# Three buffers for sums, x and v, three pairs of gates, and products five chunks behind: a long convolution beside a gated feed-forward layer

## The chip, the core and the metric

The kernel runs on one core of a Trainium2 chip. The metric is device time in microseconds (us). Three runs of the kernel before the change took 3942.79, 3947.40 and 3949.95 us; the median is 3947.4 us.

## The reference

Two blocks follow each other. B is 4, S is 12480, D is 128, the hidden width DFF is 2048; everything is float32.

```python
# block 1: a long convolution with a gate
h_filt = (np.maximum(pos_emb @ w1, 0.0) @ w2) * np.exp(-0.01 * pos)[:, None]
u = x * v
y = irfft(rfft(u, n=2*S) * rfft(h_filt, n=2*S))[:S]      # along the sequence, per column
z = x * y
# block 2: on the 49920 rows of z
h = z @ w_in                 # 128 -> 2048
out = (h * np.cos(h)) @ w_out   # 2048 -> 128
```

## The kernel before

**The convolution** is a Fourier transform written as matrix products in stages. For each of the four batches there are a first stage (f1, `f1_units`, 64 units), a second with the product by the filter's transform (f2, `f2_units`, 48 units), a third (i1, `i1_units`, 64 units) and a last (i2, `i2_units`, 30 units). Each i2 unit reads one tile `tm` of 312 KB from DRAM, multiplies the result by x (`i2_out`, L518, on VectorE) and stores it in `zd`. While i2 of batch b runs, `u_units` makes u = x*v of batch b+1: per unit it loads `xt` and `vt` (L385), multiplies in two halves (L404) and writes sums and differences into `slots` (L410). All of that arithmetic is GpSimd's (POOL). All DMAs are issued by SyncE (SP), in order, so an issue that waits holds up every later one.

**The feed-forward layer** (`moe_*`) runs beside the convolution from 343 us on. Rows come in 97 tiles of 128 x 4, and each tile has 16 chunks of 128 hidden columns; 1552 chunks in all. Chunk i is: the product with w_in (`moe_up`, L132, into a PSUM bank `ph`), a rounding on ScalarE (ACT, L753), a subtraction on VectorE (DVE, L754), a sine on ACT (L759) and a product on DVE (L760) that gives the gate `gt`. The product with w_out is a Strassen-like scheme on pairs of chunks: `moe_sums` makes four sums `ts` of a pair on POOL (L768, L771, L772), and `moe_down` multiplies gates and sums by seven combinations of weights (L785): the first half of a pair into `acca` (three products, the last of them from the sum made by L771), the second into `accb` (four products). After a tile's last pair `moe_evict` combines the accumulators into `ot`; `moe_back` transposes them into `ob`, `moe_store` writes them out. `moe_load` reads a tile of z into `zb`, `moe_turn` transposes it into `at`.

**The order** is written out by hand (`manual_schedule`, L985 to L1017). Step i issues `moe_up` of chunk i, then `moe_down` of chunk i - LAG (LAG is 6), then the sine and product of chunk i-1, then, where chunk i-1 closes a pair, its sums; then transposes if they are due (in at chunk 3, out at chunk 8). After that it issues pieces of convolution as long as these are owed:

```python
            owed += 1.0
            while owed > 0.0:
                owed -= next(conv, owed)
```

An f2 unit counts for 2.9 steps, an i2 unit for 3.5 steps in batch 0, for 3.0 in batches 1 and 2 and for 1.5 in batch 3. When the convolution has run out (at about 3160 us), the rest of the chunks runs alone; I call this the tail. There every second `ph` comes from the convolution's PSUM banks (`late`).

**Buffers.** `gt` has four pairs, `ts` two, `zb`, `ot` and `ob` one each. PSUM: `acca` and `accb` take a bank each, `ph` three; the convolution has two banks in batch 0 and three afterwards. In f2 the scratch `t` has one buffer. In `u_units`, a `bufs` of 2 gives two `xt` and one `vt`; the loads of a unit are issued `bufs - 2` units ahead.

Of the kernel before, what the change touches and what calls it, by code (L numbers as in the profile page):

```python
# [9 lines left out]
F32 = mybir.dt.float32  # L10
# [7 lines left out]
P = 128  # L18
# [15 lines left out]
def kernel(  # L34
# [71 lines left out]
    NROWS = B * NG * R  # L106
    NALL = 1 + math.ceil((NROWS - R) / P)
    assert G == 2 * UA and H % UA == 0 and N2 % G == 0
    LAG = 6
    WCOL = 256  # L110

    dram = ctx.enter_context(tc.tile_pool(name="dram", bufs=1, space=DRAM))
# [351 lines left out]
    def f2_product(pool, ps, h, k1, whole):  # L464


        y = parts[0:N2, :, k1:k1 + 2, :, :].rearrange("p r k b i -> p r b (k i)")
        t = pool.tile([N2, 2, CB, 4], F32, name="t", bufs=1 + whole)
        uu = ps[0:N2, :].rearrange("p (r b j) -> p r b j", r=2, j=4)
        if whole:  # L470
            for r, (dst, hh) in enumerate(((y, h[:, :, :, :]), (t[:, :, :, :], h[:, ::-1, :, :]))):
                u = uu[:, r]
                twice = bass.AP(tensor=u.tensor, offset=u.offset,
                                ap=[u.ap[0], [0, 2], *u.ap[1:]])
                nc.vector.tensor_tensor(dst, twice, hh, op=ALU.mult)  # L475
                yield
        for r, op in ((0, ALU.subtract), (1, ALU.add)):
            if not whole:
                nc.vector.tensor_tensor(y[:, r], uu[:, 0], h[:, r], op=ALU.mult)
                yield  # L480
                nc.vector.tensor_tensor(t[:, r], uu[:, 1], h[:, 1 - r], op=ALU.mult)
            nc.gpsimd.tensor_tensor(y[:, r], y[:, r], t[:, r], op=op)  # L482
            yield
# [83 lines left out]
    def u_units(b, bufs, u, engine, side="left"):  # L567

        with tc.tile_pool(name="xv", bufs=bufs, side=side) as pool:
            tiles = {}  # L570

            def before(j):
                tiles[j] = u_load(pool, bufs, b, j * UA)

            def after(j, _):
                for half in range(2):
                    u_multiply(tiles[j], half, engine(j, half))
                    yield
                if j == H // UA - 2:
                    clear_gap(u)  # L580
                u_sums(u, tiles.pop(j), j * UA, (nc.gpsimd, nc.gpsimd if b else nc.vector))
                yield

            yield from units(H // UA, U_STEPS, before, lambda j, ps, i: None, after, 3,
                             ahead=bufs - 2)
# [107 lines left out]
    def inverse_units(bank, b):  # L693

        if b + 1 == B:
            yield from i2_units(bank, b, 3)
            return
        new = u_units(b + 1, 2, slots[0:R, :, :, :],  # L700
                      lambda j, half: nc.gpsimd,
                      side="right" if b else "left")
        parts = 4 if b == 0 else 2
        for i, steps in enumerate(i2_units(bank, b, 2)):
            if i > 2 * parts:
                for _ in range(i % parts > 0 if b == 0 else 1 + i % 2):
                    next(new, None)
            yield steps * (FIRST_STEPS if b == 0 else I2U_STEPS) / I2_STEPS
        yield from new
# [18 lines left out]

    def moe_load(pool, n):
        m, row = rows_of(n), first_row(n)  # L730
        zb = pool.tile([P, G, D], F32, name="zb", bufs=1)
        nc.sync.dma_start(zb[0:m, :, :], zd[row:row + m, :, :])
        zbs[n] = zb

    def moe_turn(pool, n):
        m = rows_of(n)
        zb = zbs.pop(n)
        pt = ps_h.tile([P, BANK], F32, name="ph")
        for i in range(G):
            transpose(pt[:, i * m:(i + 1) * m], zb[0:m, i, :], ident)  # L740
        at = pool.tile([D, BANK], F32, name="at")
        nc.scalar.copy(out=at[:, 0:G * m], in_=pt[:, 0:G * m])
        ats[n] = at
# [18 lines left out]
    def moe_sums(pool, n, gt):  # L762

        half = G // 2 * rows_of(n)
        ts = pool.tile([P, 4, BANK // 2], F32, name="ts")
        t = [ts[:, i, 0:half] for i in range(4)]
        b11, b21 = gt[:, 0, 0:half], gt[:, 1, 0:half]
        nc.gpsimd.tensor_tensor(  # L768
            ts[:, 0:2, 0:half], gt[:, :, half:2 * half],
            gt[:, 0, 0:2 * half].rearrange("p (h n) -> p h n", h=2), op=ALU.subtract)  # L770
        nc.gpsimd.tensor_tensor(t[2], t[1], b11, op=ALU.add)  # L771
        nc.gpsimd.tensor_tensor(t[3], b21, t[2], op=ALU.subtract)  # L772
        return b11, b21, gt[:, 1, half:2 * half], t
# [16 lines left out]
    def moe_evict(pool, n, second, ot=None):  # L790
        r = rows_of(n)
        acc = sums.pop((n, second))

        def twice(a):
            return bass.AP(tensor=a.tensor, offset=a.offset, ap=[a.ap[0], [0, 2], a.ap[1]])

        if not second:
            ot = pool.tile([P, 6, P], F32, name="ot", bufs=1)
            nc.scalar.copy(out=ot[:, 2, 0:r], in_=acc[:, 0, 0:r])
            nc.vector.tensor_tensor(ot[:, 0:2, 0:r], acc[:, 1:3, 0:r], twice(ot[:, 2, 0:r]),  # L800
                                    op=ALU.add)
            return ot
        nc.vector.tensor_tensor(ot[:, 2:4, 0:r], acc[:, 0:2, 0:r], twice(ot[:, 0, 0:r]),
                                op=ALU.add)
        nc.vector.tensor_tensor(ot[:, 4:6, 0:r], acc[:, 2:4, 0:r], ot[:, 2:4, 0:r], op=ALU.add)
        nc.vector.tensor_tensor(ot[:, 0, 0:r], acc[:, 1, 0:r], ot[:, 2, 0:r], op=ALU.add)
        return ot

    def moe_back(pool, n, ot):
        m = rows_of(n)  # L810
        pt = ps_h.tile([P, BANK], F32, name="ph")
        places = pt[:, :].rearrange("p (h i e d) -> p h e i d", h=2, e=2, d=CB)
        for i, block in enumerate((1, 4, 5, 0)):
            transpose(places[0:m, i // 2, i % 2], ot[:, block, 0:m], ident)
        ob = pool.tile([P, 2, UA * D], F32, name="ob", bufs=1)
        nc.scalar.copy(out=ob[0:m, :, :].rearrange("p h n -> p (h n)"), in_=pt[0:m, :])
        return ob

    def moe_store(n, ob):
        row = first_row(n)  # L820
        while row < first_row(n + 1):
            b, g, n1 = row // R // NG, row // R % NG, row % R
            count = min(R - n1, first_row(n + 1) - row)
            first, _, second, _ = n2s(g)
            start = out[b * S + n1 * N2 + first, :]
            at = row - first_row(n)
            nc.sync.dma_start(
                bass.AP(tensor=start.tensor, offset=start.offset,
                        ap=[[N2 * D, count], [(second - first) * D, 2], [1, UA * D]]),
                ob[at:at + count, :, :])  # L830
            row += count

    with tc.manual_schedule():
# [143 lines left out]
        def load(n):  # L977
            while made[0] * R < first_row(n + 1):
                next(conv)
            moe_load(mpool, n)  # L980
# [4 lines left out]
        steps = [(n, c) for n in range(NALL) for c in range(NFC)]  # L985
        hidden, pairs, gates, ots, obs = {}, {}, {}, {}, {}
        for i in range(len(steps) + LAG):
            if i < len(steps):
                n, c = steps[i]
                if n == 0 and c == NFC // 2:  # L990
                    load(1)
                if c == NFC - 4 and n + 2 < NALL:
                    load(n + 2)
                if c % 2 == 0:
                    pairs[i] = mpool.tile([P, 2, BANK], F32, name="gt", bufs=4)
                hidden[i] = moe_up(mpool, n, c, pairs[i - c % 2])
            if i >= LAG:
                pn, pc = steps[i - LAG]
                moe_down(pn, pc // 2, pc % 2, *gates[i - LAG - pc % 2])
                if pc >= NFC - 2:  # L1000
                    ots[pn] = moe_evict(mpool, pn, pc % 2, ots.get(pn))
            if 0 <= i - 1 < len(steps):
                moe_act(*hidden.pop(i - 1))
                pn, pc = steps[i - 1]
                if pc % 2:
                    gates[i - 2] = moe_sums(mpool, pn, pairs.pop(i - 2))
            if i < len(steps):

                if c == (3 if n else NFC - 2) and n + 1 < NALL:
                    moe_turn(mpool, n + 1)  # L1010
                if c == NFC // 2 and n - 1 in ots:
                    obs[n - 1] = moe_back(mpool, n - 1, ots.pop(n - 1))
                if c == NFC // 2 + 2 and n - 1 in obs:
                    moe_store(n - 1, obs.pop(n - 1))
# [3 lines that stand above are left out]
# [30 lines left out]
```

## Time and profile before

| quantity | value |
|---|---|
| median of three runs | 3947.4 us |
| the profiled execution, its own time | 3949.47 us |
| its span (first to last instruction) | 3947.6 us |
| TensorE (PE) busy | 3703.9 us (94%) |
| DVE busy | 2903.3 us (74%) |
| POOL busy | 2838.1 us (72%) |
| ACT busy | 2281.0 us (58%) |
| mean granted clock of PE | 0.983 |

Busy time is an average over stages that are limited by different things, so it has to be read by stage: 350 to 610 us is i2 of batch 0, 620 to 1205 us is f1, f2 and i1 of the next batch, 1215 to 1505 us its i2, and so on; 3020 to 3160 us is the last i2 and from there on the tail. The profile names a wait by the instruction that waits and the one that released it. The end of a matmul is modelled, so durations of PE are better read from start to start.

### The profile page before, as it was taken

Reading aid. Unit: us, or ns where it says so; the run is one execution under the profiler, and the core shown is the slowest. Engines: PE = TensorE matmul, PEld = TensorE weight load, DVE = VectorE, ACT = ScalarE, POOL = GpSimd, SP = SyncE. Lnnn points to the kernel's source line nnn. Section 1 sums busy time; section 2 is a strip of 40 time slices with the busy share of each in tenths; the row PEclk is TensorE's granted clock in tenths of the full one; section 3 lists DMA queues with packets and bytes.
Section 4 is the critical chain, followed back from the end, with each engine's and each line's share of the span. In section 5 each row is a group of like instructions: output and inputs, shape, how many; then the busy total and the mean of one; then the engine's idle time right before and its main releaser. Section 6 shows DMA issues by size and latency. Waiting matters only on the chain.

```text
span 3947.6 us, 101170 instructions
## 1 busy us (share of the span) xinstructions
PE 3703.9 (94%) x40298; PEld 2595.6 (66%) x40298; DVE 2903.3 (74%) x5722; ACT 2281.0 (58%) x4660; POOL 2838.1 (72%) x3361
## 2 busy tenths in 40 slices
PE   7898999999999889999999889999999999999999
PEld 6776766655576656655577566655577766666666
DVE  8887777777776557787776456777777577777777
ACT  5756666655554446655555345655555367776776
POOL 7667996688746776688846776588854477878777
PEclk9999999999999999999999999999999999999999
DMA  5253541122203541122202551022202500000000
GB/s 159 78 165 114 158 142 29 36 69 73 62 13 106 141 130 36 29 71 70 66 19 79 142 145 39 24 70 73 68 23 73 163 27 18 23 20 21 23 18 19
DMA packets 209709, 279.59 MB, mean 71 GB/s; under 512 B 17111, under 2 KB 146535, under 8 KB 209111
## 3 DMA queue, kind: packets, MB, share of 16 engines
q1 hardware_dynamic: 209239, 273.12, 24.1%
q8 instruction: 320, 5.24, 0.6%
q14 instruction: 150, 1.23, 0.1%
HBM read 193.64 MB, written 79.42 MB: 69 GB/s over the span
## 4 chain that ended last, share of the span: by engine, by line
PE 67%; POOL 11%; DMA 5%; DVE 5%; issue 2%; ACT 1%; SPq 1%; POOLq 0%; ACTq 0%; DVEq 0%
PE ph L132 23%; PE cv L132 18%; PE accb L785 14%; PE acca L785 10%; DMA tm<-td 4%; POOL ts L768 4%; PE ph L136 2%; POOL ts L771 2%; POOL ts L772 2%; DVE gt L760 2%; DVE gt L754 1%; POOL xt L404 1%; POOL slots L482 1%; POOL slots L410 1%; ACT gt L753 1%
## 5 line engine op out<-in xcount | busy, mean ns | idle before, releaser
L753 ACT ACTIVATE gt<-ph 128x512 int32<-128x512 f32 (+1 forms) x1339 | 797.7, 596 | 1347.3 <-PE ph L132 1231.3
L768 POOL TENSOR_TENSOR ts<-gt 128x512 f32<-128x512 f32 (+2 forms) x784 | 998.4, 1273 | 791.4 <-PE accb L785 737.1
L754 DVE SCALAR_TENSOR_TENSOR gt<-ph,gt 128x512 f32<-128x512 f32 (+1 forms) x1339 | 918.9, 686 | 791.1 <-ACT gt L753 779.3
L132 PE MATMUL ph<-at,w_in_sb 128*64 128x512 f32 (+1 forms) x5356 | 1414.0, 601 | 78.6 <-DVE gt L760 56.8
L759 ACT ACTIVATE gt<-gt 128x512 f32<-128x512 f32 (+1 forms) x1568 | 973.8, 621 | 32.1 <-DVE gt L754 32.1
L760 DVE TENSOR_TENSOR gt<-ph,gt 128x512 f32<-128x512 f32 (+1 forms) x1339 | 907.4, 678 | 0.3
L785 PEld LDWEIGHTS acca<-gt,w_out_sb 128*64 128x64 f32 x6272 | 410.0, 137 | 435.7 <-issue 425.3
L785 PE MATMUL accb<-ts,w_out_sb 128*64 128x128 f32 (+2 forms) x9408 | 655.1, 273 | 0.0
L772 POOL TENSOR_TENSOR ts<-gt,ts 128x256 f32<-128x256 f32 (+2 forms) x784 | 571.1, 728 | 61.5
L771 POOL TENSOR_TENSOR ts<-ts,gt 128x256 f32<-128x256 f32 (+2 forms) x784 | 570.6, 728 | 61.5
L785 PEld LDWEIGHTS accb<-ts,w_out_sb 128*64 128x64 f32 x9408 | 549.3, 138 | 0.0
L785 PEld LDWEIGHTS accb<-gt,w_out_sb 128*64 128x64 f32 x3136 | 236.7, 137 | 439.3 <-issue 437.3
L132 PEld LDWEIGHTS ph<-at,w_in_sb 128*64 128x64 f32 x5356 | 362.8, 138 | 186.1 <-issue 50.9
L785 PE MATMUL acca<-gt,w_out_sb 128*64 128x128 f32 (+2 forms) x6272 | 483.3, 273 | 0.0
L132 PE MATMUL cv<-slots,tm 96*40 96x128 f32 (+1 forms) x3840 | 286.6, 293 | 88.4 <-DMA tm<-td 81.8
L482 POOL TENSOR_TENSOR slots<-slots,t 120x256 f32<-120x256 f32 x384 | 278.9, 737 | 57.9 <-DVE t L475 35.9
L785 PE MATMUL acca<-ts,w_out_sb 128*64 128x128 f32 (+1 forms) x3136 | 311.7, 273 | 2.3 <-POOL ts L771 2.1
L785 PE MATMUL accb<-gt,w_out_sb 128*64 128x128 f32 (+1 forms) x3136 | 312.4, 273 | 0.0
L132 PEld LDWEIGHTS cv<-slots,tm 96*40 96x40 f32 (+1 forms) x3840 | 240.0, 130 | 106.8 <-DMA tm<-td 92.7
L132 PE MATMUL cv<-at,w_in_sb 128*64 128x512 f32 (+1 forms) x916 | 234.7, 591 | 0.0
L404 POOL TENSOR_TENSOR xt<-xt,vt 104x256 f32<-104x256 f32 x228 | 169.4, 750 | 68.4 <-DMA vt<-in_v_dram 65.0
L785 PEld LDWEIGHTS acca<-ts,w_out_sb 128*64 128x64 f32 x3136 | 205.2, 138 | 3.1 <-POOL ts L771 3.1
(145 smaller groups left out, 4109.6 us busy)
## 6 DMA issues: line engine op xcount, KB each, us to landing
h<-hd SPq DMA_DIRECT2D x144, 240.0 KB
tm<-td SPq DMA_DIRECT2D x96, 312.0 KB
xt<-in_x_dram SPq DMA_DIRECT2D x120, 208.0 KB
vt<-in_v_dram SPq DMA_DIRECT2D x120, 208.0 KB
xs<-in_x_dram SPq DMA_DIRECT2D x120, 208.0 KB
zd<-xs SPq DMA_DIRECT2D x119, 208.0 KB
zb<-zd SPq DMA_DIRECT2D x96, 256.0 KB
w<-wd SPq DMA_DIRECT2D x144, 116.2 KB
```

The costliest lines, as they stand in the source:

```text
L132: nc.tensor.matmul(dst[lo:hi], left[:, lo:hi], right, start=start, stop=stop)
L136: nc.tensor.transpose(dst, src, ident[0:n, 0:n])
L404: engine.tensor_tensor(xt[:, half, :], xt[:, half, :], vt[:, half, :], op=ALU.mult)
L482: nc.gpsimd.tensor_tensor(y[:, r], y[:, r], t[:, r], op=op)
L753: nc.scalar.activation(turns, ph[:, 0:m], AF.Identity, bias=phase)
L754: nc.vector.scalar_tensor_tensor(out=part, in0=ph[:, 0:m], scalar=phase, in1=turns, op0=ALU.add, op1=ALU.subtract)
L759: nc.scalar.activation(part, part, AF.Sin, scale=scale)
L760: nc.vector.tensor_tensor(part, ph, part, op=ALU.mult)
L768: nc.gpsimd.tensor_tensor(ts[:, 0:2, 0:half], gt[:, :, half:2 * half], gt[:, 0, 0:2 * half].rearrange("p (h n) -> p h n", h=2), op=ALU.sub ...
L771: nc.gpsimd.tensor_tensor(t[2], t[1], b11, op=ALU.add)
L772: nc.gpsimd.tensor_tensor(t[3], b21, t[2], op=ALU.subtract)
L785: nc.tensor.matmul(acc[h * CB:(h + 1) * CB, place, 0:r], w_out_sb[:, pair, weight, :], right[:, h * r:(h + 1) * r], start=(pair == 0 and i ...
```

## The change

It does the following:

- `LAG` is 5, and within a step `moe_down` (with `moe_evict`) is issued ahead of `moe_up`; `gt` has three pairs, `ts` three buffers.
- `t` in f2 has two buffers.
- `u_units` of the later batches gets `bufs=3`: three `xt`, two `vt`, and loads one unit ahead.
- The transposes in are issued at chunk 8, directly ahead of the transposes out, and take a PSUM bank of the convolution.
- `zb` and `ob` share one buffer (`tile`); `ot` has four blocks in place of six, and the evictions of `accb` are reordered so that the last adds in place.

```diff
-    LAG = 6
+    LAG = 5
...
-        t = pool.tile([N2, 2, CB, 4], F32, name="t", bufs=1 + whole)
+        t = pool.tile([N2, 2, CB, 4], F32, name="t", bufs=2)
...
-        new = u_units(b + 1, 2, slots[0:R, :, :, :],
+        new = u_units(b + 1, 3, slots[0:R, :, :, :],
...
-        zb = pool.tile([P, G, D], F32, name="zb", bufs=1)
+        zb = pool.tile([P, G, D], F32, name="tile", bufs=1)
...
-        pt = ps_h.tile([P, BANK], F32, name="ph")
+        pt = bank()
...
-        ts = pool.tile([P, 4, BANK // 2], F32, name="ts")
+        ts = pool.tile([P, 4, BANK // 2], F32, name="ts", bufs=3)
...
-            ot = pool.tile([P, 6, P], F32, name="ot", bufs=1)
+            ot = pool.tile([P, 4, P], F32, name="ot", bufs=1)
...
-        nc.vector.tensor_tensor(ot[:, 4:6, 0:r], acc[:, 2:4, 0:r], ot[:, 2:4, 0:r], op=ALU.add)
         nc.vector.tensor_tensor(ot[:, 0, 0:r], acc[:, 1, 0:r], ot[:, 2, 0:r], op=ALU.add)
+        nc.vector.tensor_tensor(ot[:, 2:4, 0:r], acc[:, 2:4, 0:r], ot[:, 2:4, 0:r], op=ALU.add)
...
-        for i, block in enumerate((1, 4, 5, 0)):
+        for i, block in enumerate((1, 2, 3, 0)):
...
-        ob = pool.tile([P, 2, UA * D], F32, name="ob", bufs=1)
+        ob = pool.tile([P, G, D], F32, name="tile", bufs=1)
...
         for i in range(len(steps) + LAG):
+            if i >= LAG:
+                pn, pc = steps[i - LAG]
+                moe_down(pn, pc // 2, pc % 2, *gates[i - LAG - pc % 2])
+                if pc >= NFC - 2:
+                    ots[pn] = moe_evict(mpool, pn, pc % 2, ots.get(pn))
             if i < len(steps):
...
-                if c == NFC - 4 and n + 2 < NALL:
+                if c == (NFC - 4 if n else NFC - 1) and n + 2 < NALL:
                     load(n + 2)
                 if c % 2 == 0:
-                    pairs[i] = mpool.tile([P, 2, BANK], F32, name="gt", bufs=4)
+                    pairs[i] = mpool.tile([P, 2, BANK], F32, name="gt", bufs=3)
                 hidden[i] = moe_up(mpool, n, c, pairs[i - c % 2])
-            if i >= LAG:
-                pn, pc = steps[i - LAG]
-                moe_down(pn, pc // 2, pc % 2, *gates[i - LAG - pc % 2])
-                if pc >= NFC - 2:
-                    ots[pn] = moe_evict(mpool, pn, pc % 2, ots.get(pn))
...
-                if c == (3 if n else NFC - 2) and n + 1 < NALL:
+                if c == (NFC // 2 if n else NFC - 2) and n + 1 < NALL:
                     moe_turn(mpool, n + 1)
```

More of the change, by code (lines that the diff above doesn't have):

```diff
@@ L812, in moe_back @@
         places = pt[:, :].rearrange("p (h i e d) -> p h e i d", h=2, e=2, d=CB)
-        for i, block in enumerate((1, 4, 5, 0)):
+        for i, block in enumerate((1, 2, 3, 0)):
             transpose(places[0:m, i // 2, i % 2], ot[:, block, 0:m], ident)
-        ob = pool.tile([P, 2, UA * D], F32, name="ob", bufs=1)
-        nc.scalar.copy(out=ob[0:m, :, :].rearrange("p h n -> p (h n)"), in_=pt[0:m, :])
+        ob = pool.tile([P, G, D], F32, name="tile", bufs=1)
+        nc.scalar.copy(out=ob[0:m, :, :].rearrange("p g d -> p (g d)"), in_=pt[0:m, :])
         return ob
@@ L829, in moe_store @@
                         ap=[[N2 * D, count], [(second - first) * D, 2], [1, UA * D]]),
-                ob[at:at + count, :, :])
+                ob[at:at + count, :, :].rearrange("p (h n) d -> p h (n d)", h=2))
             row += count
@@ L987 @@
         for i in range(len(steps) + LAG):
[L988 to L991, printed above, removed]
-                if c == NFC - 4 and n + 2 < NALL:
-                    load(n + 2)
-                if c % 2 == 0:
-                    pairs[i] = mpool.tile([P, 2, BANK], F32, name="gt", bufs=4)
-                hidden[i] = moe_up(mpool, n, c, pairs[i - c % 2])
             if i >= LAG:
@@ L1001 @@
                     ots[pn] = moe_evict(mpool, pn, pc % 2, ots.get(pn))
+            if i < len(steps):
+                n, c = steps[i]
+                if n == 0 and c == NFC // 2:
+                    load(1)
+                if c == (NFC - 4 if n else NFC - 1) and n + 2 < NALL:
+                    load(n + 2)
+                if c % 2 == 0:
+                    pairs[i] = mpool.tile([P, 2, BANK], F32, name="gt", bufs=3)
+                hidden[i] = moe_up(mpool, n, c, pairs[i - c % 2])
             if 0 <= i - 1 < len(steps):
```

## The prediction

> **What bounds the kernel now.** I read busy time by stage first. Columns: stage, its length, busy time of PE, weight loads, DVE, ACT and POOL, PE's granted clock, DMA share, GB/s.
>
> ```profile
> 350.00:610.00 260.00, 244.81 (x2925) 175.50 (x2923) 188.87 (x346) 170.04 (x355) 242.82 (x309) 0.99 0.47 143
> 1215.00:1505.00 290.00, 245.57 (x2808) 176.95 (x2806) 154.20 (x255) 120.18 (x218) 218.45 (x270) 0.96 0.47 133
> 1665.00:1965.00 300.00, 279.01 (x2834) 174.89 (x2832) 237.85 (x484) 161.09 (x290) 248.15 (x294) 1.00 0.25 71
> 3180.00:3880.00 700.00, 700.00 (x7554) 449.68 (x7552) 551.14 (x921) 492.23 (x895) 559.09 (x612) 1.00 0.07 21
> ```
>
> The tail (last line) is all PE, as are f1 and i1 (no idle PE from 1100 to 1200 us). PE idles in f2 (third line, 21 of 300 us) and most in i2 of batches 1 and 2 (second line, 44 of 290); i2 of batch 0 is full on POOL (243 of 260). So the change can gain in i2 and f2, and in the tail it can only lose.
>
> Next, the timeline in the tail, for the way from a gate to its product with w_out:
>
> ```profile
> 3502.30 1.03 PE L132 MATMUL ph<-at,w_in_sb 128*64 128x512 f32 x4
> ...
> 3503.43 0.60 ACT L753 ACTIVATE gt<-ph 128x512 int32<-128x512 f32 x1 [0.68 <-PE ph L132]
> ...
> 3503.59 0.39 PE L785 MATMUL acca<-ts,w_out_sb 128*64 128x128 f32 x4
> ...
> 3504.06 0.69 DVE L754 SCALAR_TENSOR_TENSOR gt<-ph,gt 128x512 f32<-128x512 f32 x1 [0.51 <-ACT gt L753]
> ...
> 3504.67 0.68 DVE L760 TENSOR_TENSOR gt<-cv,gt 128x512 f32<-128x512 f32 x1
> ```
>
> (The L760 here works on the odd chunk before, whose bank is a cv.) From the starts on PE in this stretch (3502.30, 3503.16, 3503.81, 3504.67, 3505.54) an up product takes 0.86 us, a first half 0.65, a second half 0.87: 3.24 per pair. Transposes repeat every 27.44 us, which leaves 27.44 - 8 x 3.245 = 1.48 us per tile for them.
>
> Then the waits in f2 (total, times, longest), and the chain of waits in i2:
>
> ```profile
> DVE t L481 <- POOL slots L482: 38.1, 28, 2.6
> ...
> PE ph L132 <- DVE gt L760: 16.9, 18, 2.9
> ```
>
> ```profile
> 1376.34 1.30 POOL ts L768
> ...
> 1384.17 0.70 POOL xt L404
> ...
> 1385.78 4.40 DMA tm<-td
> ...
> 1390.22 1.92 PE cv L132 x15
> ...
> 1394.82 1.29 POOL ts L768
> ```
>
> In f2, DVE stands behind POOL for the only `t`, and PE then behind DVE for a `ph` bank. In i2, POOL makes sums, writes u, multiplies, makes sums, multiplies; the last multiplication frees `vt`, SP issues `vt`, `xs` and only then `tm`, PE waits for `tm`, and POOL's next sums wait until PE has freed a `ts` (accb). One round is 1394.82 - 1376.34 = 18.48 us for two i2 units; over 24 units (1245.78 to 1464.90) the mean is 9.13 us per unit.
>
> **Term 1: the shorter lag, in the tail.** By the order of instructions, a pair's first half stood behind the up product that opens the third pair after it and now stands behind that of the second. One whole pair, 3.24 us, of slack goes. What is left is counted from the start U of the up product that closes the way to the sums: ACT at U+1.13, L754 at +1.76, L760 at +2.37, ending +3.05; POOL starts 0.14 later (as in most starts of L768 that DVE releases), L771 starts 1.36 after L768 and takes 0.73; PE starts 0.05 after L771 (at 3938.95, where it waited for it). The sum is there at U+5.33. PE arrives at 0.86+0.65+0.86+0.87+0.86+0.43 = U+4.53. So it stalls 0.80 us, with the next up products queued behind. In the steady state two pairs take 5.33+0.22+0.86+0.87 = 7.28, 3.64 per pair and not 3.24. The transposes lie inside such a wait and hide it once per tile, and the evictions of accb (1.1 us from start to start on DVE, ahead of L754) add 0.7 to one wait per tile. Stepping through the eight pairs: 4.72+3.24+4.04+3.24+4.04+3.24+4.04+3.94 = 30.5 us per tile against 27.44, that is +3.06 on 27 tiles (3155 to 3896 us): **+83 us**. Ends: without the eviction's part 2.36 per tile (+64); at 3.64 for all eight pairs, plus 1.48 and 0.7, 31.3 (+104). I take 83: each link is a row of this stage.
>
> f1 and i1 have about 0.8 to 1.0 us of convolution per chunk: PE needs 9.6 us or more for two pairs, the way 7.28+0.9: **0**; if DVE and ACT add 1.5 us there, the cover is gone.
>
> **Term 2: f2.** 139 chunks per batch (48 x 2.9) take 2.25 us each (count of L753 between 1660 and 1900). PE alone would need 1.715 (27.44/16) plus 0.30 (a unit has as many columns as an up product, 0.86, spread over 2.9 steps) = 2.01. The second `t` takes away the 38 us wait, since the buffer was then read a whole unit (6 us) earlier; a third `ts` takes away POOL's wait for accb (26.6 us). What is late next is the short lag: 7.28+0.30 = 7.58 for two pairs against PE's 7.68, so any delay of the sums over 0.1 us shows. POOL has 2.85 us of sums and one or two L482 of 0.74 per pair of 4.0 us, so sums can be 0.3 late; with evictions and the transposes out (they still take a `ph` bank) I take 2.13 per chunk: 0.12 x 139 x 3 = **-50 us**. Ends: 2.05 (-83) and, with sums 1 us late, 2.25 (0).
>
> **Term 3: i2 beside u.** The changed order on SP is the same, `xt`, `vt`, `xs`, `tm`, and `vt` still waits for the second multiplication of the unit before. But that comes earlier: `vt` is loaded a unit ahead (POOL waited 23.2 us for it here), and sums wait for the gate and not for accb (37.7 us). The new round for two units: U to sums 3.19; sums 2.84; multiplication, `vt`, `xs` to `tm` 1.65; `tm` to PE 4.87 (mean of 18 such waits, 4.2 to 5.9); from there to the next U 1.03+0.65+0.86+0.87 = 3.41. Together 15.96, 7.98 per unit; with stores and tile loads on SP (0.8 and 0.4 us per 5.3 units, about a third of it in the round, and the tile load now also waiting for the store) I take 8.3. (9.13-8.3) x 27 units x 2 batches = 45; what is left of u after i2 no longer waits for `vt`, about 2 us for each of two batches: **-49 us**. Ends: PE's own 7.5 per unit (-92) and 8.9 (-13). Batch 0 is full on POOL: **-5** (0 to -10).
>
> A part of that is the clock. The product after a wait of 2.29 us took 1.92 us and those after 2.79, 3.73 and 4.43 us 1.97, against 1.2 after 3.33 (the granted clock was 0.57 to 0.72 there, 0.96 and 0.94 over the two stages). The Trainium skill ("TensorE: Matmul & The Clock Gate", Part 1) has PE drop to half clock after an idle window of some 3.4 us that runs free. By the page alone waits under 3.4 us would cost nothing in clock; by the rows, 2.29 is enough. My round has waits of about 1 us, below both, so the sum is the same by either.
>
> **The rest, costed at nothing.** Transposes in: the same four products, in a bank of the convolution that is free for ACT's 0.6 us copy; they no longer take a `ph` bank (PE waited 3 to 4 us per f2 stage for the copy out of one). Shared `tile`: the load stands two steps (3.4 us) behind the store in SP's queue and is needed 12 chunks later; a store lands in about 4 us (zd<-xs), so SP may hold later loads by some 0.6 us, counted above. `gt` with three pairs: its last reader now stands directly ahead of the up product. The evictions are as many as before; ACT's copy of acca (0.27 us) now stands ahead of L753, but the up product that L753 waits for takes longer. The drain at the end waits for POOL in either.
>
> **Sum:** 83 - 50 - 49 - 5 = -21 on 3949.47 (span 3947.6; 1.9 lie around it). The median is 2.1 below that execution, so 3926.
>
> **Rivals.** *The lag decides (slower).* The place is PE's wait for `ts` at acca (L785) in f2, too. If sums start 1 us late on the mean there, f2 runs at (7.58+1.0)/2 = 4.29 per pair plus transposes, about 2.25 per chunk, and gains 0; with i2 at 8.9 per unit the time is 83-13-5: 4012. It decides from f2 above 2.19 per chunk with i2 at 8.4 (-25, -43, -5: +10). For it: at 2.13 per chunk POOL would be busy 248/300 x 2.25/2.13 = 87% in f2 and DVE 84%. Against: no wait of PE for POOL there now, and DVE's longest stalls go.
>
> *All stalls of the convolution go (much faster).* f2 at 2.05, i2 at PE's 7.5: 83-83-92-5 = -97: 3850. Against: `tm` still waits behind `vt`.
>
> *i2 does not change,* since SP's order is as before: 83-50-5 = +28: 3975. Against: in the chain shown, POOL waits for accb ahead of both multiplications.
>
> *The terms cancel* within 8 us (0.2%, about what a measurement of this kernel can tell from no change): 3947.
>
> **Chances.** Net gain as forecast (by more than 8 us, down to 3885) 0.40; much faster 0.10; cancel 0.13; i2 unchanged 0.15; the lag decides 0.22. That is faster 0.50, same 0.13, slower 0.37. The forecast's own range is 3885 to 3939. The range 3878 to 3992 leaves out most of the much faster case and the far half of the lag's.
>
> **What would show it.** In the changed profile: tiles in the tail at 30.5 us, with PE waiting for POOL L771 at acca about 0.8 us on every second pair; no DVE wait for L482 and 2.13 us per chunk in f2; no POOL wait for `vt` or accb, PE's waits for `tm` at about 1 us and a clock of 0.99 in i2. A tail still at 27.4 us per tile would break term 1 and make it 83 us faster; f2 above 2.19 or i2 above 8.8 would make the change a loss.

## The result, and the profile after

The changed kernel takes 3965.7 us (median of eight runs, 3958.13 to 3973.44), the kernel before 3945.89 beside it (eight runs): a ratio of 1.0037, 95% interval 1.002 to 1.0054. It is slower by 0.4%, where 3926 and "faster" were forecast. The profiled execution took 3973.44 us, its span 3971.6, that is 24.0 more than the span before.

Busy time by stage, in the same four windows and columns as before:

```profile
350.00:610.00 260.00, 245.29 (x2932) 176.10 (x2930) 187.54 (x342) 167.21 (x352) 234.73 (x298) 0.99 0.48 144
1215.00:1505.00 290.00, 253.06 (x2844) 184.54 (x2841) 159.24 (x265) 123.28 (x231) 222.43 (x274) 0.94 0.46 131
1665.00:1965.00 300.00, 294.43 (x3134) 187.23 (x3132) 254.03 (x516) 169.47 (x318) 252.84 (x300) 1.00 0.24 70
3180.00:3880.00 700.00, 646.04 (x6818) 402.47 (x6820) 502.62 (x830) 436.75 (x807) 505.37 (x555) 1.00 0.07 19
```

In f2 (third line) PE's idle time fell from 21 to 5.6 us and it did 3134 matmuls in place of 2834. In the tail (last line) PE, full before, idles 54 of 700 us and does 6818 in place of 7554. The second i2 (second line) still has a low clock, 0.94. POOL was busy for 243 of 260 us in the first i2 and is for 235 now (first line), and that stage became longer all the same.

Cut at the first product of each stage, the two profiled executions differ as follows (us; sums over the batches for f1, f2 and i1):

| stage | before | after | difference | forecast |
|---|---|---|---|---|
| start-up | 338.0 | 339.0 | +1.1 | 0 |
| i2 of batch 0 | 270.8 | 278.3 | +7.4 | -5 |
| f1 | 418.3 | 434.8 | +16.5 | 0 |
| f2 | 965.3 | 902.4 | -62.9 | -50 |
| i1 | 437.2 | 438.9 | +1.7 | 0 |
| i2 of batches 1 and 2 | 587.4 | 559.6 | -27.8 | -49 |
| last i2 and tail | 927.6 | 1015.3 | +87.7 | +83 |
| sum | | | +23.7 | -21 |

The tail does what was worked out for it. PE's timeline (start, length, what, and in brackets its wait):

```profile
3565.68 1.03 PE L132 MATMUL ph<-at,w_in_sb 128*64 128x512 f32 x4
3566.54 0.61 PE L785 MATMUL acca<-gt,w_out_sb 128*64 128x128 f32 x8
3567.77 0.44 PE L785 MATMUL acca<-ts,w_out_sb 128*64 128x128 f32 x4 [0.62 <-POOL ts L771]
...
3569.77 1.03 PE L132 MATMUL ph<-at,w_in_sb 128*64 128x512 f32 x4
...
3573.01 1.03 PE L132 MATMUL ph<-at,w_in_sb 128*64 128x512 f32 x4
...
3575.11 0.44 PE L785 MATMUL acca<-ts,w_out_sb 128*64 128x128 f32 x4 [0.63 <-POOL ts L771]
```

From `ph` to `ph` the pairs take 4.09 and 3.24 us in turn (the step by step count had 4.04 and 3.24), and PE waits for L771 in every second one. Transposes in stand at 3316.02 and 3407.37, three tiles apart: 30.45 us per tile, against the 30.5 forecast. In f2 DVE's wait for L482 is gone; what is left runs the other way, and PE waits a little for sums (waits of 1665 to 1965 us: total, times, longest):

```profile
PE acca L785 <- POOL ts L771: 5.0, 13, 0.7
...
POOL slots L482 <- DVE t L481: 3.7, 7, 0.7
```

In the first i2, where no such wait stood before, the same wait appears (345 to 620 us):

```profile
PE acca L785 <- POOL ts L771: 10.7, 12, 2.1
```

In f1 PE begins to wait for the evictions of the convolution's banks (1490 to 1635 us; in the same stage before, L425 alone with 1.5 us):

```profile
PE cv L132 <- DVE slots L425: 3.7, 12, 0.5
...
PEld cv L132 <- ACT slots L423: 3.4, 6, 0.6
```

And in the second i2 (1215 to 1505 us in both), SP's queue and PE's waits for `tm`. Before:

```profile
SPq L385 <- POOL xt L404: 127.5, 29, 10.1
SPq L385 <- POOL slots L410: 57.5, 15, 7.8
```

```profile
PE cv L132 <- DMA tm<-td: 35.6, 18, 4.6
```

After:

```profile
SPq L385 <- POOL xt L404: 148.6, 28, 11.2
SPq L385 <- POOL slots L410: 27.1, 12, 3.5
```

```profile
PE cv L132 <- DMA tm<-td: 30.6, 14, 4.0
```

POOL no longer waits for `vt`, nor for accb. But SP still waits for POOL's multiplications (L404) before it can issue a `vt`: 148.6 us now, 127.5 before. Its waits for an `xt` (L410) became shorter, and all its waits at L385 together take 182 us now and 198 before. The order on SP shows who stands behind the wait for `vt` (start, length):

```profile
1344.07 0.33 SPq L385 DMA_DIRECT2D xt<-in_x_dram  x1
1348.06 0.33 SPq L385 DMA_DIRECT2D vt<-in_v_dram  x1
1348.43 0.81 SPq L827 DMA_DIRECT2D out_dram<-tile  x2
1349.34 0.40 SPq L385 DMA_DIRECT2D xs<-in_x_dram  x1
1349.84 0.38 SPq L681 DMA_DIRECT2D tm<-td  x1
```

`vt` waits from 1344.4 until POOL's L404 (1347.30, 0.73 us) is through, and `tm`, which needs nothing of that, is issued at 1349.84. PE waits for it until 1355.83.

### The profile page after: what moved, and what is told of

Read it like the earlier page. It is cut to its first block, busy times and chain, and to the rows that moved or that the text cites. A ratio compares the mean times of both kernels' runs of the same rounds, so it can differ in the third digit from the quotient of the medians.

```text
span 3971.6 us, 101626 instructions
## 1 busy us (share of the span) xinstructions
PE 3710.7 (93%) x40298; PEld 2590.1 (65%) x40298; DVE 2918.0 (73%) x5722; ACT 2237.4 (56%) x4660; POOL 2834.9 (71%) x3361
## 4 chain that ended last, share of the span: by engine, by line
PE 53%; POOL 13%; DVE 12%; DMA 5%; ACT 4%; issue 3%; SPq 1%; ACTq 0%; POOLq 0%; DVEq 0%
PE ph L132 18%; PE cv L132 15%; PE accb L785 11%; PE acca L785 7%; POOL ts L768 6%; DVE gt L754 4%; DVE gt L760 4%; POOL ts L771 4%; DMA tm<-td 4%; ACT gt L753 3%; PE cv L136 1%; POOL ts L772 1%; DMA zd<-xs 1%; PE ph L136 1%; POOL xt L404 1%
## 5 line engine op out<-in xcount | busy, mean ns | idle before, releaser
L753 ACT ACTIVATE gt<-ph 128x512 int32<-128x512 f32 (+1 forms) x1339 | 797.5, 596 | 1400.5 <-PE ph L132 1328.5
L754 DVE SCALAR_TENSOR_TENSOR gt<-ph,gt 128x512 f32<-128x512 f32 (+1 forms) x1339 | 920.0, 687 | 818.1 <-ACT gt L753 813.1
L132 PE MATMUL ph<-at,w_in_sb 128*64 128x512 f32 (+1 forms) x5356 | 1396.2, 595 | 8.2 <-DVE gt L760 3.9
L771 POOL TENSOR_TENSOR ts<-ts,gt 128x256 f32<-128x256 f32 (+2 forms) x784 | 570.0, 727 | 61.5
L785 PEld LDWEIGHTS acca<-gt,w_out_sb 128*64 128x64 f32 x6272 | 399.6, 138 | 220.0 <-issue 180.3
L785 PE MATMUL acca<-ts,w_out_sb 128*64 128x128 f32 (+1 forms) x3136 | 323.1, 281 | 100.6 <-POOL ts L771 98.6
L132 PEld LDWEIGHTS cv<-slots,tm 96*40 96x40 f32 (+1 forms) x3840 | 248.0, 130 | 209.1 <-DMA tm<-td 110.0
L132 PEld LDWEIGHTS ph<-at,w_in_sb 128*64 128x64 f32 x5356 | 350.1, 138 | 19.0 <-ACT tile L816 6.8
L482 POOL TENSOR_TENSOR slots<-slots,t 120x256 f32<-120x256 f32 x384 | 278.2, 739 | 44.9 <-DVE t L475 27.7
L785 PEld LDWEIGHTS acca<-ts,w_out_sb 128*64 128x64 f32 x3136 | 190.6, 137 | 150.4 <-POOL ts L771 148.4
L754 DVE SCALAR_TENSOR_TENSOR gt<-cv,gt 128x512 f32<-128x512 f32 (+1 forms) x229 | 156.6, 684 | 140.0 <-ACT gt L753 139.8
```

Of the source, the lines that this page charges most:

```text
L132: nc.tensor.matmul(dst[lo:hi], left[:, lo:hi], right, start=start, stop=stop)
L753: nc.scalar.activation(turns, ph[:, 0:m], AF.Identity, bias=phase)
L754: nc.vector.scalar_tensor_tensor(out=part, in0=ph[:, 0:m], scalar=phase, in1=turns, op0=ALU.add, op1=ALU.subtract)
L785: nc.tensor.matmul(acc[h * CB:(h + 1) * CB, place, 0:r], w_out_sb[:, pair, weight, :], right[:, h * r:(h + 1) * r], start=(pair == 0 and i ...
```

## The experiments

Each kernel was timed beside the kernel before on the same chip, which took 3950 to 3953 us there; ratios are to that, with their 95% intervals. Stage lengths (us) come from each kernel's profiled execution, cut as above:

| kernel | time | i2, batch 0 | f1 | f2 | i1 | i2, batch 1 | i2, batch 2 | last i2 and tail |
|---|---|---|---|---|---|---|---|---|
| before | 3946 | 270.8 | 418.3 | 965.3 | 437.2 | 288.2 | 299.2 | 927.6 |
| after | 3966 | 278.3 | 434.8 | 902.4 | 438.9 | 280.7 | 278.9 | 1015.3 |
| e2 before, five behind, down first | 4001 | 275.9 | 433.7 | 943.5 | 438.6 | 282.0 | 285.1 | 1005.8 |
| e3 after, transposes in in `ph` | 4042 | 281.5 | 444.4 | 930.8 | 453.8 | 286.8 | 295.1 | 1014.2 |
| e5 before, `ts` 3, `t` 2 | 3852 | 270.8 | 419.5 | 908.3 | 437.2 | 268.2 | 273.9 | 927.8 |
| e7 before, `t` 2, x and v 3 and 2 | 3890 | 272.0 | 417.9 | 908.9 | 437.2 | 293.2 | 295.8 | 928.7 |
| e9 after, x and v 2 and 1 | 3979 | 276.4 | 435.0 | 904.1 | 438.9 | 283.4 | 285.8 | 1012.6 |
| e10 after, `ts` 2 | 3970 | 278.7 | 434.6 | 902.9 | 438.9 | 277.6 | 280.2 | 1010.7 |
| e11 as e5, five behind, up first | 3868 | 272.5 | 419.3 | 910.9 | 436.9 | 277.9 | 281.5 | 933.4 |
| e12 after, six behind, x and v 2 and 1 | 3828 | 270.4 | 412.0 | 892.4 | 435.7 | 274.3 | 277.8 | 920.7 |
| e13 as e5, transposes in in a `cv` | 3846 | 270.3 | 417.8 | 900.6 | 439.2 | 271.9 | 279.0 | 929.4 |
| e14 as e5, transposes in at chunk 8 | 3845 | 270.5 | 419.3 | 903.0 | 445.4 | 265.9 | 277.0 | 919.1 |
| e15 as e12, x and v 2 and 2 | 3751 | 268.3 | 411.4 | 892.4 | 435.7 | 234.9 | 244.4 | 916.7 |
| e16 as e5, both of e13 and e14 | 3810 | 269.5 | 410.6 | 889.6 | 435.2 | 269.2 | 276.0 | 917.3 |
| e17 before, x and v 2 and 2 | 3863 | 269.6 | 418.9 | 965.3 | 438.7 | 244.9 | 255.4 | 924.8 |
| e18 after, x and v 2 and 2, no lead | 3895 | 274.7 | 433.1 | 903.2 | 438.9 | 241.9 | 247.7 | 1011.2 |
| e19 after, x and v 3 and 3, lead of one | 3892 | 274.7 | 433.2 | 902.7 | 438.9 | 238.2 | 246.6 | 1014.0 |

### The lag and the order of the step

**e2: the lag alone.** In the kernel before:

```diff
-    LAG = 6
+    LAG = 5
...
+            if i >= LAG:
+                pn, pc = steps[i - LAG]
+                moe_down(pn, pc // 2, pc % 2, *gates[i - LAG - pc % 2])
...
             if i < len(steps):
...
-                    pairs[i] = mpool.tile([P, 2, BANK], F32, name="gt", bufs=4)
+                    pairs[i] = mpool.tile([P, 2, BANK], F32, name="gt", bufs=3)
...
-            if i >= LAG:
-                pn, pc = steps[i - LAG]
-                moe_down(pn, pc // 2, pc % 2, *gates[i - LAG - pc % 2])
...
```

> The kernel before with one part of the change alone: products five chunks behind, ahead of the chunk's first products, and three pairs of gates. Buffers, transposes and loads stay as before. Theory A (the shorter lag is what costs, and the order of the step with it): the tail takes 1015 us from the last i2 on, as in the changed kernel, against 927 (+88); each f1 takes 143 to 147 us against 139 to 141 (+16 in all), because down now stands ahead of up and the evictions of the convolution queue behind a later up; the first i2 +7. Sum 3946 + 88 + 16 + 7 = 4057, or less by what f2, with its one product buffer, already waits for elsewhere. Theory B (the lag costs in the tail alone; what f1 lost is the bank that a tile's transposes in now take from the convolution): the tail 1015, f1 at 139 to 141, sum 4034.

Measured: 4001.23 us, ratio 1.0115 (1.0099 to 1.0131). The tail grew by 78, f1 by 15.4, the first i2 by 5, near A's 88, 16 and 7, with the transposes in their old place: f1's loss comes with the lag and the order, not with the bank. The total fell short of 4057 since neither theory had what this edit gives: with the one `t` and two `ts` of before, f2 became 22 us shorter and the later i2 20. Sums whose products come earlier are read earlier, so their buffers may come free earlier; this is a reading that no run tests by itself.

**e11: five behind, up first.** As e5 (below), with one edit more:

```diff
-    LAG = 6
+    LAG = 5
```

> Before with three buffers for sums and two for the product, and products five chunks behind, but still after the chunk's own first product (up, then down; four pairs of gates). Theory A (it is the order that costs: down ahead of up makes PE ask for the pair's differences 0.87 us sooner, at U+4.53 where they are ready at U+5.33; behind the up it asks at U+5.40): the tail after the last i2 stays at 787 to 797 us, f1 at 139 to 141, total 3852 to 3862. Theory B (five chunks behind costs, whichever stands first): the tail 850 to 872, f1 143 to 147, total 3930 to 3950.

Measured: 3868.06, ratio 0.979 (0.977 to 0.981). From the last i2 unit on it takes 790.6 us (before 787.2, after 871.8); f1 takes 419.3. PE is full again in the tail (3100 to 3800 us):

```profile
3100.00:3800.00 700.00, 700.00 (x7526) 447.08 (x7524) 552.26 (x918) 487.40 (x891) 554.58 (x610) 1.00 0.07 20
```

So A: five behind alone costs the tail and f1 next to nothing; it is the one up product of 0.86 us that no longer stands ahead of the pair's products that takes them. No run has down first with six behind, so this is the price of the order at five behind. By the count, PE asks 0.07 us after the sum is there with it, and 0.80 us before without it. What five behind still costs is 17 us in the later i2 (278 and 282 against e5's 268 and 274), which A did not have; why is open.

### The buffers

**e5: three `ts` and two `t`.** In the kernel before:

```diff
-        t = pool.tile([N2, 2, CB, 4], F32, name="t", bufs=1 + whole)
+        t = pool.tile([N2, 2, CB, 4], F32, name="t", bufs=2)
...
-        ts = pool.tile([P, 4, BANK // 2], F32, name="ts")
+        ts = pool.tile([P, 4, BANK // 2], F32, name="ts", bufs=3)
```

> The kernel before with the two buffers alone that bear on f2: three buffers for sums (ts) and two for the product (t). Lag, order and x/v buffers stay. Theory A (the buffers earn in f2 what the changed kernel shows there, whatever the lag): f2 takes 299 to 303 us per batch against 319 to 324 (-63 in all), nothing else moves by more than 5, total 3883. Theory B (the gain in f2 came with the order of the step, down ahead of up, which lets POOL start earlier): f2 keeps 310 or more, total 3915 or more.

Measured: 3851.98, ratio 0.9735 (0.9719 to 0.975). f2 fell by 57, near A's 63, so the gain needs no new order; but the later i2 fell as well, by 20 and 25 us, which neither theory had.

**e7: two `t`, more x and v.** In the kernel before:

```diff
-        t = pool.tile([N2, 2, CB, 4], F32, name="t", bufs=1 + whole)
+        t = pool.tile([N2, 2, CB, 4], F32, name="t", bufs=2)
...
-        new = u_units(b + 1, 2, slots[0:R, :, :, :],
+        new = u_units(b + 1, 3, slots[0:R, :, :, :],
```

> The kernel before with two buffers for the product (t) and three for x and v (xt 3, vt 2); the sums keep two buffers, and lag, order and transposes stay as before. Theory A (the product's buffer alone earns f2's gain, x and v's buffers alone earn i2's): f2 299 to 303 us per batch (-63), i2 of the two later batches 281 and 279 against 288 and 299 (-28), or better, since the load of a tile stays where it was; total 3855, under both kernels. Theory B (f2's gain needs the third buffer for sums, POOL's sums then no longer waiting for the second products): f2 stays near 320, total 3918. Theory C (i2's gain is the order's or the lag's): i2 stays at 288 and 299, total 3883.

Measured: 3890.44, ratio 0.9839 (0.9821 to 0.9856). f2 is e5's to 0.6 us: its gain is the second `t` alone. The later i2 are at 293 and 296, that is +1.6 in all: C. Three and two buffers for x and v earn nothing there, and POOL waits for accb as before, only longer (1201 to 1494 us):

```profile
POOL ts L768 <- PE accb L785: 68.4, 22, 7.6
```

In e5 this wait is gone from i2, and POOL starts on its sums when the gate is there (1196 to 1464 us):

```profile
POOL ts L768 <- DVE gt L760: 18.9, 11, 3.4
```

So with six behind the third `ts` is worth the 45 us of i2, as far as e7 speaks for the second `t` alone (no run has that by itself).

**e9 and e10: one buffer of the changed kernel undone each.**

```diff
-        new = u_units(b + 1, 3, slots[0:R, :, :, :],
+        new = u_units(b + 1, 2, slots[0:R, :, :, :],
```

> The changed kernel with two buffers for x and one for v again (u_units of the later batches with 2, not 3). Theory A (x and v's third buffer earned nothing; i2's gain is the third buffer for sums): i2 of the two later batches stays within 5 us each of 281 and 279, total 3966 within 8. Theory B (beside three buffers for sums the x and v loads do become the next thing late): i2 goes up by 10 to 20 us each, total 3986 to 4006.

Measured: 3978.91, ratio 1.0066 (1.0045 to 1.0087); the later i2 took 2.7 and 6.9 us more. Between the two theories, nearer A in i2: about 10 us is what x and v's buffers earn in the changed kernel.

```diff
-        ts = pool.tile([P, 4, BANK // 2], F32, name="ts", bufs=3)
+        ts = pool.tile([P, 4, BANK // 2], F32, name="ts", bufs=2)
```

> The changed kernel with two buffers for sums. Theory A (the third buffer is what the i2 of the later batches and little else use: before with three for sums and two for the product had i2 20 and 25 us shorter than before, before with two for the product and three for x and v did not): i2 280 to 295 us each, +5 to +15, f2 within 5 us of 300 each, the tail +0 to +10, total 3976 to 4000. Theory B (with products only five behind, the buffer of sums two pairs back is given up before the next sums need it, so that a third is never used): nothing moves by more than 3, total 3966.

Measured: 3969.99, ratio 1.0045 (1.0028 to 1.0062), no stage but the last more than 3.1 us from the changed kernel's: B. The third `ts`, which the kernel before could have used, earns nothing in the changed one. What took i2 down by 28 there would then be the shorter lag with its order (20, e2) and some 10 of x and v's buffers (e9); that the two add up so is not tested.

### The transposes

**e3: transposes in back in `ph`.** In the changed kernel:

```diff
-        pt = bank()
+        pt = ps_h.tile([P, BANK], F32, name="ph")
```

> The changed kernel, but a tile's transposes in go back to a bank of the chunks' own (ph) instead of one of the convolution's three. Theory A (f1 lost its 16 us to the order of the step): f1 stays at 143 to 147 us, the total within 4 us of the changed kernel's 3966. Theory B (f1 lost them to the bank): f1 returns to 139 to 141 us, the waits of PE for the evictions of L425 and L423 in f1 go from 5 to 7 us per batch to under 2, and the total falls by 12 to 16, to 3950 to 3954. If the first i2's 7 us were the bank's as well, another 7 less.

Measured: 4042.13, ratio 1.0212 (1.0192 to 1.0233). Neither: the time rose by 76 us (69 by the ratios), in f1, f2, i1 and the later i2. The transposes in and out are issued one behind the other, and now the second waits for ACT's copy (L742) of the first (whole span):

```profile
PE ph L136 <- ACT at L742: 72.2, 68, 1.2
```

On the timeline it is this, with the rest of the step behind it:

```profile
1738.79 0.66 PE L136 MATMUL ph<-ident,tile 128*128 128x128 f32 x4
...
1740.61 0.66 PE L136 MATMUL ph<-ident,ot 128*128 128x128 f32 x4 [1.17 <-ACT at L742]
```

In the changed kernel the second transposes started 0.49 us after the first (1745.47, 1745.96). The bank that the forecast costed at nothing is what makes the new place bearable.

**e12: the changed kernel, six behind.** Up ahead of down, and, since the fourth pair of gates takes their room, x and v with two and one:

```diff
-    LAG = 5
+    LAG = 6
...
-        new = u_units(b + 1, 3, slots[0:R, :, :, :],
+        new = u_units(b + 1, 2, slots[0:R, :, :, :],
...
-            if i >= LAG:
-                pn, pc = steps[i - LAG]
-                moe_down(pn, pc // 2, pc % 2, *gates[i - LAG - pc % 2])
...
-                    pairs[i] = mpool.tile([P, 2, BANK], F32, name="gt", bufs=3)
+                    pairs[i] = mpool.tile([P, 2, BANK], F32, name="gt", bufs=4)
                 hidden[i] = moe_up(mpool, n, c, pairs[i - c % 2])
+            if i >= LAG:
+                pn, pc = steps[i - LAG]
+                moe_down(pn, pc // 2, pc % 2, *gates[i - LAG - pc % 2])
...
```

> The changed kernel with products six chunks behind again, up ahead of down and four pairs of gates, and x and v with two and one buffers (memory has no room for the third beside the fourth pair). What stays of the change: three buffers for sums, two for the product, the transposes in and out together at chunk 8 with the in-transposes in a convolution bank, the shared tile, the smaller ot. Theory A (the transposes' rearrangement is worth nothing by itself): total 3852 within 6, as before with the two buffers alone. Theory B (a convolution bank taken at chunk 8 costs the convolution): f1, f2 and i1 together 5 to 20 us longer, 3857 to 3872. Theory C (it frees a bank of the chunks' own and helps, as its loss cost the changed kernel 76 us when the in-transposes went back to ph): 3800 to 3845.

Measured: 3827.75, ratio 0.9689 (0.9671 to 0.9706): C. Against e5, which has the same buffers, lag and order, it is 24 us faster, in f2 (-16), f1 (-7.5) and the tail (-7), while the later i2 took 10 us more. The rearranged transposes come here with the shared `tile` and the smaller `ot`.

**e13, e14, e16: bank and place apart.** On e5, the first edit alone, the second alone, and both:

```diff
-        pt = ps_h.tile([P, BANK], F32, name="ph")
+        pt = bank()
...
-                if c == (3 if n else NFC - 2) and n + 1 < NALL:
+                if c == (NFC // 2 if n else NFC - 2) and n + 1 < NALL:
```

> Before with three buffers for sums and two for the product, six chunks behind, and a tile's transposes in still at chunk 3, but in a convolution bank. Theory A (what helps is a bank of the chunks' own left to the ups, wherever the transposes stand): f1, f2 and i1 together 20 to 30 us shorter than with the two buffers alone, the tail 7, total 3820 to 3835. Theory B (it is the pair of transposes one behind the other that helps): total 3845 to 3855, as with the two buffers alone.

> The same two buffers, six behind, and the transposes in stand at chunk 8 right ahead of those out, both in banks of the chunks' own. Theory A (the two one behind the other in ph hold two of the three ph banks at once, as in the changed kernel with the in-transposes in ph, which lost 76 us): total 3900 to 3930 against 3852. Theory B (that loss belongs to five behind with down first; with six behind the banks suffice): total within 6 of 3852.

> Before with the parts that earned: three buffers for sums, two for the product, and the transposes in at chunk 8 in a convolution bank; six behind, up first, separate buffers for a tile's load and its store, the larger ot. Theory A (the shared tile makes its load wait for the store on SP's queue, ahead of the inverse tables, and that is why i2 took 274 and 278 us with it against 268 and 274 without): i2 268 and 274, the rest as with the shared tile, total 3816 to 3820, the fastest of all. Theory B (i2's 5 us each come from the transposes at chunk 8): i2 274 and 278, total 3828.

Measured: 3846.18 (0.9721, 0.9697 to 0.9745), 3844.83 (0.9725, 0.9706 to 0.9744) and 3810.05 (0.9641, 0.9617 to 0.9665), against 0.9735 for e5. The bank alone and the place alone are worth little each (B both times, e14 a shade faster than B's 6 us allow): f2 -8 and -5, the place also -9 in the tail and +8 in i1. Both together give f2 -19, f1 -9, the tail -10. With six behind and up first, e3's wait of the second transposes for the first one's copy (in e14 46.4 us in all) costs nothing that shows in the total. e16 and e12 differ by the separate buffers for a tile's load and store (and the larger `ot`): the later i2 are 5 and 2 us shorter, which goes A's way, but not all of the 18 us between them lie there.

### The loads of v

**e15: e12 with a second `vt`.** Two and two, no lead:

```diff
-        for name, src, n in (("xt", x, bufs), ("vt", v, bufs - 1)):
+        for name, src, n in (("xt", x, bufs), ("vt", v, 2)):
```

> The changed kernel with six behind, up first, four pairs of gates, and two buffers for x and two for v (memory has room for these). Theory A (POOL's waits for v in i2, 19 us in a batch, are not what sets i2; PE's waits for the inverse tables are): i2 stays at 274 and 278 us, total within 5 of 3828. Theory B (v's single buffer sets when POOL ends and so when PE goes on): i2 5 to 10 us shorter each, total 3808 to 3818.

Measured: 3750.66, ratio 0.9486 (0.9466 to 0.9505), 5% under the kernel before and the fastest of all. The later i2 fell by 39 and 33 us, several times what B had, and PE, whose clock is 0.95 in e12's second i2 (1189 to 1463 us), runs there with an almost full one (1200 to 1430 us):

```profile
1200.00:1430.00 230.00, 222.83 (x2685) 165.52 (x2682) 150.55 (x250) 117.19 (x215) 214.67 (x266) 0.99 0.56 159
```

This left open why three and two buffers earned so little in the changed kernel.

**e17, e18, e19: v alone, without the lead, with a third `vt`.** The same edit in the kernel before (e17); the same edit in the changed kernel with `u_units(b + 1, 2, ...)` (e18); and, in the changed kernel with its lead of one unit (e19):

```diff
-        for name, src, n in (("xt", x, bufs), ("vt", v, bufs - 1)):
+        for name, src, n in (("xt", x, bufs), ("vt", v, bufs - 1 if b == 0 else bufs)):
```

> The kernel before with one edit: two buffers for v beside two for x in the later batches, loaded for the unit in hand (no lead). Theory A (SP's wait for v's buffer, with the inverse table's load queued behind it, is what makes PE wait in i2): PE's waits for the inverse table go from 36 us in the second i2 to under 8, i2 falls from 288 and 299 to 240 to 260 each, total 3952 - 80 within 20, 3852 to 3892. Theory B (two buffers for sums keep POOL, and with it PE, as late as now): i2 275 or more, total 3925 or more.

> The changed kernel with two buffers for x and two for v and no lead, in place of three and two with a lead of one unit: a buffer less. Theory A (the lead uses up the buffer that the change adds: a load of v for the next unit still finds both taken, and SP waits at it): i2 falls from 281 and 279 to 235 to 250 each, total 3966 - 70 within 15, 3881 to 3911. Theory B (with products five behind and down first, i2 is bound elsewhere): i2 275 or more, total 3958 or more.

> The changed kernel with three buffers for v as well as for x in the later batches, and the lead of one unit kept. Theory A (it is the number of v buffers against the lead): SP's wait for POOL's multiply goes as with two and two without a lead, i2 235 to 250 each, total 3881 to 3911. Theory B (it is the lead: x and v of the next unit are put on the queue ahead of the inverse table, whichever buffers there are): i2 270 or more, total 3950 or more.

Measured: 3863.2 (0.9777, 0.976 to 0.9795), 3894.8 (0.9859, 0.9844 to 0.9874), 3892.46 (0.9854, 0.9839 to 0.9869). A in all three. e18 has one `xt` fewer than the changed kernel and is 71 us faster. In its second i2 (1200 to 1440 us) SP waits for `xt`, after the sums of L410, and no longer for L404 and `vt`, and PE hardly waits for `tm`:

```profile
SPq L385 <- POOL slots L410: 91.8, 28, 16.6
```

```profile
PE cv L132 <- DMA tm<-td: 4.1, 3, 3.0
```

What counts is the buffers less the lead. Before, the load of `vt` for unit j needed the buffer that unit j-1 was still multiplying. In the changed kernel the load stands a unit earlier, but it is that of unit j+1, it has two buffers, and so it waits for the same multiplication of unit j-1 at the same place in SP's queue. Two without a lead (e18) or three with it (e19) wait for unit j-2, which is long done.

The Trainium skill ("DMA: Bandwidth & Descriptors", Anatomy of one DMA) says that a DMA's semaphore wait happens on the issuing sequencer before dispatch; the rows of SP above agree (L385 148.6 us in the changed kernel, `tm` issued only after it).

## Why the prediction was wrong

**Term 1, the tail: right.** +83 forecast, +87.7 measured (4 of it still in the last i2), with the pairs and the tile that the count had. PE waits for L771's sum in every second pair, as was named, and with up first (e11), where by the count it arrives after the sum, the loss is gone.

**f1 costed at nothing: wrong, +16.5.** The forecast had PE needing 9.6 us for two pairs there and the way 8.2, and named the point at which that cover goes (1.5 us more on DVE and ACT). e2 (+15.4) and e11 (+1.0) show that the order of the step takes the time. How is argued only: with down first, the convolution's products follow directly on the up that L753 and L754 wait for, and their evictions queue behind those. Waits for evictions make 3.7 + 3.4 us of the stage quoted; another part is weight loads for `cv` that wait for PE itself (9.0 us there, 2.5 in the same stage before). Waits at acca are not it: in the three f1 stages of the changed kernel they make at most 0.9 us.

**The first i2: wrong sign, +7.4 for -5.** POOL was indeed relieved, but 10.7 us of PE's waits at acca came in. e2 lost 5 us there with 10.6 of this wait, e11 (up first) 1.7 us with 4.3 of it, and with six behind (e5, e12) it is not there. The forecast looked for the short lag's wait in f2 and the tail, not here.

**Term 2, f2: right, too small.** -62.9 for -50: 902.4 us over 427 chunks is 2.11 per chunk, where 2.13 was forecast and 2.05 was the lower end. The mechanism was half right: the second `t` is nearly all of it (-57 in e5, -56 in e7), the third `ts` none (e7, e10). What was "late next", the sums, shows as 5 us in a stage.

**Term 3, the later i2: the step that failed.** -27.8 for -49; over the same units as the forecast's 9.13, the pace beside u was 8.89 us per unit in batch 1 and 8.56 in batch 2 (before 9.13 and 9.30) for 8.3. The forecast said itself that `vt` still waits for the multiplication of the unit before, ahead of `tm`, and then let that wait shrink, because the multiplication would come earlier. It came earlier by less than 1 us. From a unit's first product to the issue of the next unit's `tm` it is 3.0 us in batch 1 and 3.2 in batch 2 (mean of the 24 units from the seventh on), 4.0 and 3.9 before, and 1.0 and 1.4 in e18. The gain was therefore short, and the wait stayed: SP arrives at `vt` sooner and waits there longer, 148.6 us for 127.5. The forecast's words for what would show the term right were no POOL wait for `vt` or accb (true), waits for `tm` at about 1 us (2.2 on the mean: 30.6 by 14) and a clock of 0.99 (0.94 in batch 1, 0.97 in batch 2). The first is met and the others are not, so those waits of POOL were not what set the round. e9 prices the x and v buffers at 10 us, e10 the third `ts` at nothing, and e17 to e19 show the wait that did set it: with a third `vt` as the only edit to the changed kernel (e19) i2 takes 238 and 247 us.

**The rest at nothing: not shown.** Transposes at chunk 8 in `ph` would have cost about 70 us (e3), and the convolution's bank avoids that; with six behind, place and bank together earn about 40 (e16 against e5, 0.9641 for 0.9735). No run has the changed kernel with its transposes in at chunk 3, so what the two are worth together five behind is open.

**The sum.** Of the 45 us between -21 and +24, f1 is 16.5, the first i2 12, the later i2 21, the tail 5, start-up and i1 3; f2 gives back 13. Of the rivals, none came as it was told: f2 did not slow down, and i2 did change, but by a little over half of the term. That the rival without a change in i2 gave 3975, near the 3966 measured, is luck: i2 lost 28 us that it did not have, and f1 and the first i2 took 24 more, which no case had.

## What to carry to other kernels

Count buffers less lead: a deeper prefetch with one buffer more waits for the same reader as before, and where one queue issues everything in order, the wait to look for is the queue's own, with the list of what stands behind it. A lag is a distance in an engine's instructions, so moving one instruction across another can use up the slack that a buffer buys; and a buffer's worth depends on the lag (the third `ts` is worth 45 us six behind with up first, nothing five behind with down first), so price parts in the order in which they will stand. Here the changed kernel's three `ts`, two `t` and new transposes, put six chunks behind with up first again and given a second `vt` with no lead, turn a loss of 0.4% into a gain of 5% (e15).

## What the runs showed of the hardware

How long a wait must be to halve PE's clock was open in the forecast. In the changed kernel's second i2, an up product after a wait of 1.77 us took 1.94 us, one after 1.22 us 1.05:

```profile
1330.49 1.34 PE L132 MATMUL cv<-slots,tm 96*64 96x128 f32 x16 [1.77 <-DMA tm<-td]
...
1332.88 1.94 PE L132 MATMUL ph<-at,w_in_sb 128*64 128x512 f32 x4
...
1355.83 1.21 PE L132 MATMUL cv<-slots,tm 96*64 96x128 f32 x16 [1.22 <-DMA tm<-td]
...
1357.73 1.05 PE L132 MATMUL ph<-at,w_in_sb 128*64 128x512 f32 x4
```

Six of the profiles (before, after, e2, e9, e12, e18) have 230 waits of PE for `tm` of more than 0.15 us; the length of the next up product shows what the clock did: it is 1.02 to 1.06 us or, slowed, 1.20 to 1.95. Of 150 waits under 1.7 us, none was followed by a slowed one; of 51 between 1.7 and 3.4, 24 were; of 29 over 3.4, 28. That is what a free-running window of about 1.7 us would give: a wait of two windows always holds a whole one, a shorter one only sometimes. It is an inference from the counts, and not the only one: a window of 3.4 us in which half of the time idle is enough would give the same limits, and no run here tells the two apart. The window in the Trainium skill ("TensorE: Matmul & The Clock Gate", Part 1), cited in the forecast, is one of 3.4 us. If all of it had to be idle, the 24 would not be slow.
